# Moving the routing steps of a mixture-of-experts kernel inside its attention stage

## The chip, the cores and the metric

The kernel runs on one core of a Trainium2 chip. A core has five engines that work side by side: TensorE (matrix products, PE in the rows), VectorE (DVE), ScalarE (ACT), GpSimd (POOL) and SyncE (SP), and 16 DMA engines. Each engine takes its instructions strictly in the order of its own queue; an instruction whose operands are not ready holds all that is queued behind it. The metric is the device time of one execution in microseconds.

## The reference

Three stages in a row. The first is a gated linear attention over 4 batches, 8 heads, 768 positions and 48 columns a head:

```python
for t in range(S):
    state = alpha[:, :, t, :, None] * state + k_t (x) v_t
    y[:, :, t] = q_t . state
```

Its output is a matrix of 3072 tokens by 384. The second stage sends each token to two of 8 experts: `logits = x @ w_gate`, plus `log1p(exp(x @ w_noise)) * noise`; the two largest of each token are taken, a softmax over the two gives their weights, and the output is the weighted sum of `relu(x @ w1[e]) @ w2[e]` (384 to 1024 to 384). The third is `(x @ w_a * (x @ w_b)) @ w_out` (384 to 1536 to 384).

## The kernel before

**Attention.** Time is cut in 24 chunks of 128 tokens, six to a batch. In a chunk `i` TensorE does, in this order: the transposes of the next chunk's keys (`t_unit`, line 665), the transposes of the previous chunk's output for the gate (`gx_unit`, line 763), the product of the carried state with the queries (`inter`, line 701; none in the first chunk of a batch), the next chunk's scores (`sc_unit`, lines 681 and 682), masked scores by values (`intra`, line 710), the gate products (`gm_unit`, line 772) and the products of the next state (`u_unit`, line 739). VectorE masks the scores (line 685; the mask is applied to blocks of 128 rows by 64 columns on the diagonal), and makes the two scans of the decays three chunks ahead (`prep`, lines 641 and 645). GpSimd multiplies keys and queries by them (lines 643 and 646), then multiplies the state by its decay (line 755, in `s_unit`), and splits one chunk of expert weights in two parts (line 116). ScalarE copies the output, the state into the layout that `inter` reads (`sbd`, line 728), the masks' result (lines 690 and 692) and transposes out of PSUM.

From chunk `FILL` on, a product of constants (128x128 by 128x512, bf16, line 629) is put ahead of the key transposes and ahead of the gate transposes.

**Routing** is written as Python generators that are advanced by `tick`. There are four ticks in a chunk: 0 behind the transposes, 1 behind the scores and `prep`, 2 behind the masked values and gate products, 3 behind the state. A `yield` ends the generator's share of a tick, so that the number of yields between two steps says how many ticks lie between them. What a step issues goes into the engines' queues at that place of the program. Behind the attention there are two more ticks, then two in each up product (`up_unit`) of the first expert and one in each quarter of a down product.

Tokens are routed in two groups, chunks 0 to 13 and 14 to 23. The second group's choice is made in two parts (chunks 14 to 18, 19 to 23). For a group, `choose` computes the noisy logits and the two best experts, `route` ranks the tokens within each expert with a scan and products of triangular masks (lines 346 to 352), and finds with one-hot products (line 394) the token numbers of expert 0's rows; `gather` (line 494) fetches these rows with an indirect DMA issued by GpSimd, so that `x_unit(0, 0)` to `x_unit(0, 2)` (line 502) can transpose them in and behind chunk 23. `lists` does the same with one-hot products (line 461) for the other experts, in sets of five tiles. `before_states` holds a step that uses TensorE until tick 2 of a chunk, or until no chunk is running.

The first group's steps stand in these places (chunk.tick):

| step | engine | before |
|---|---|---|
| softplus: abs, exp, log, ... | ScalarE | 14.3, 15.0, 15.1 |
| three products, two products | GpSimd | 15.3, 16.0 |
| sum, best and second expert | VectorE | 17.0 to 18.1 |
| sum of both choices; scan | GpSimd; VectorE | 18.2; 19.0 |
| ranks | TensorE | 20.2 |
| rank arithmetic, masks of keys | VectorE | 20.3, 21.0 |
| two lane comparisons (line 385) | VectorE | 21.1, 21.2 |
| places (line 394) | TensorE | 22.2 |
| row indices; three gathers | VectorE; GpSimd | 22.3; 23.0 |
| slot products (line 408) | GpSimd | 23.1, 23.3 |
| lists | VectorE, TensorE | from the second tick behind the last chunk |

The second group's first part has its three and two GpSimd products in 20.3 and 21.0, and its comparisons in 22.0 to 23.1.

**Behind the attention** the eight experts follow, each with up products (lines 846 to 848, three products of split operands), relu and split (lines 897 and 898), and down products; then the third stage. These two take from 140 us to the end.

Of the kernel before, what the change touches and what calls it, by code (L numbers as in the profile page):

```python
# [21 lines left out]
NT = B * NCH  # L22
# [20 lines left out]
LAG = 3  # L43
# [2 lines left out]
W_LOAD = range(4, 20)  # L46
W_SPLIT = [*range(6, 22)]
WARM = 7
FILL = 13
RING = 6  # L50
BLK = 512
NB = N // BLK
# [9 lines left out]
def moe_kernel(ctx: ExitStack, tc, qka, afirst, v, wgn, noise, w1, w2, w3, out):  # L62
# [4 lines left out]
    def tl(pool, shape, dt, tag, **kw):  # L67
        uid[0] += 1
        return pool.tile(shape, dt, tag=tag, name=f"{tag}_{uid[0]}", **kw)
# [91 lines left out]
    def trbank():  # L161
        trn[0] += 1
        return bank(trn[0] % 2)
# [33 lines left out]
    def scratch(name, shape, late, dt=F32):  # L197
        if late:
            return tl(rt, [128, *shape], dt, "s_" + name)
        if name not in SMALL:  # L200
            SMALL[name] = place(shape, None, dt)
        return SMALL[name]
# [33 lines left out]
    def spot(kind, n):  # L236

        c = SPOTS[kind]
        return small[0][:, c:c + n] if small else trbank()[:, :n]

    phase = [None]

    def before_states():
        while phase[0] in (0, 1, 3):
            yield

    def choose(s):

        i0, i1 = CHS[s], CHS[s + 1]
        g, j0 = group_of[i0]  # L250
        n = i1 - i0
        sh = [128, n, E]
        last = i1 == NT

        def tmp(name):
            return tl(rt, [128, MCH, E], F32, "r_" + name)[:, :n]

        def scr(name, *shape):
            return scratch(name, (n if last else MCH, *shape), last)[:, :n]

        def hop(usual, late=0):

            return range(late if last else usual)

        eng = nc.vector if last else nc.gpsimd
        lg, z = LG[:, i0:i1, :E], LG[:, i0:i1, E:]
        az, ex, w, c, r, ln, mz, sp = (tmp(x) for x in ("az", "ex", "w", "c", "r", "ln", "mz", "sp"))
        for _ in hop(1):
            yield
        nc.scalar.activation(az, z, AF.Abs)  # L270
        nc.scalar.activation(ex, az, AF.Exp, scale=-1.0)
        nc.scalar.activation(w, ex, AF.Copy, bias=1.0)
        for _ in hop(1):
            yield
        nc.scalar.activation(ln, w, AF.Ln)
        nc.scalar.activation(r, ln, AF.Exp, scale=-1.0)
        for _ in hop(1):
            yield
        nc.scalar.activation(c, w, AF.Copy, bias=-1.0)
        nc.scalar.activation(mz, z, AF.Relu)  # L280
        for _ in hop(2, 1):
            yield
        eng.tensor_tensor(c, c, ex, op=ALU.subtract)
        eng.tensor_tensor(c, c, r, op=ALU.mult)
        eng.tensor_tensor(sp, ln, c, op=ALU.subtract)
        yield
        eng.tensor_tensor(sp, sp, mz, op=ALU.add)
        eng.tensor_tensor(sp, sp, noise_t[:, i0:i1], op=ALU.mult)
        for _ in hop(4):
            yield  # L290
        nl = scr("nl", E)
        nc.vector.tensor_tensor(nl, sp, lg, op=ALU.add)
        ms = []
        for k in range(2):
            eq = scr("eq", E)
            m, mk = (tl(rt, [128, MCH], F32, f"r_{x}{k}", bufs=2)[:, :n] for x in ("m", "mk"))
            o = oh[k][:, i0:i1]
            nc.vector.tensor_reduce(m, nl, axis=AX.X, op=ALU.max)
            for _ in hop(1):
                yield  # L300
            nc.vector.tensor_tensor(eq, nl, m[:, :, None].to_broadcast(sh), op=ALU.is_equal)
            nc.vector.tensor_tensor(eq, eq, prio[:, None, :].to_broadcast(sh), op=ALU.mult)
            for _ in hop(1):
                yield
            nc.vector.tensor_reduce(mk, eq, axis=AX.X, op=ALU.max)
            nc.vector.tensor_tensor(o, eq, mk[:, :, None].to_broadcast(sh), op=ALU.is_equal)
            yield
            if k == 0:
                nl2 = scr("nl2", E)
                nc.vector.scalar_tensor_tensor(nl2, o, -1e30, nl, op0=ALU.mult, op1=ALU.add)  # L310
                nl = nl2
            ms.append(m)
        oav = oas[g][:, :, 1:].rearrange("p e j -> p j e")[:, j0:j0 + n]
        eng.tensor_tensor(oav, oh[0][:, i0:i1], oh[1][:, i0:i1], op=ALU.add)
        eng.tensor_tensor(dm[:, i0:i1], ms[1], ms[0], op=ALU.subtract)
        for _ in hop(2, 1):
            yield

    def route(g):
# [5 lines left out]
        last = g == len(groups) - 1  # L325
# [12 lines left out]
        nc.vector.tensor_tensor_scan(xc.rearrange("p e j -> p (e j)"), d0[g].rearrange("p e j -> p (e j)"),  # L338
                                     oa.rearrange("p e j -> p (e j)"), 0.0, op0=ALU.mult, op1=ALU.add)
        carry[0] = xc[:, :, n]  # L340
        for _ in range(LAG + 1 if last else LAG):
            yield
        yield from before_states()
        pb = spot("ranks" if last else "ranks0", n * E + E + 1)
# [38 lines left out]
        for j0 in range(0, n, m):  # L383
# [2 lines left out]
                                    op=ALU.is_equal)  # L386
            ats.append(at)
            yield
        for _ in range(LAG - 1 if last else LAG):
            yield  # L390
        yield from before_states()
        pl = spot("lists" if last else "places0", NJ)
# [23 lines left out]
    def hot_tile(name, w, m):  # L416

        size = {"at": 128, "eqk": WL, "bt": WL}[name]
        t = tl(rt, [128, size * 2 * HOT], F16, name, bufs=2)
        return t[:, :w * m].rearrange("p (w t) -> p w t", t=m)  # L420

    def lists(g):

        i0, i1 = groups[g][0], groups[g][-1] + 1
        n = i1 - i0
        pi, ki, pf, kf = (tl(rt, [128, max(GROUPS), 2], dt, x)[:, :n]
                          for x, dt in (("ei", I32), ("ri", I32), ("rf", F16), ("e1", F16)))
        nc.vector.tensor_scalar(pi, slot[:, i0:i1], 127, None, op0=ALU.bitwise_and)
        nc.vector.tensor_scalar(ki, slot[:, i0:i1], 7, None, op0=ALU.logical_shift_right)
        nc.vector.tensor_copy(pf, pi)  # L430
        nc.vector.tensor_copy(kf, ki)
        sets = [(a, b) for a, b in zip(SUBS, SUBS[1:]) if i0 <= a < i1]
        hot = {}

        def make(s):
            j0, j1 = s
            m = j1 - j0
            at, eq, bt = (hot_tile(x, w_, 2 * m) for x, w_ in (("at", 128), ("eqk", WL), ("bt", WL)))
            for out_, src, val in ((at, lane, pf), (eq, keys[:, NJ:], kf)):
                w_ = src.shape[1]  # L440
                nc.vector.tensor_tensor(out_, src[:, :, :2 * m],
                                        val[:, j0 - i0:j1 - i0].rearrange("p a k -> p (a k)")[:, None, :]
                                        .to_broadcast([128, w_, 2 * m]), op=ALU.is_equal)
                yield
            nc.vector.tensor_tensor(bt, eq, token[:, j0:j1].rearrange("p a k -> p (a k)")[:, None, :]
                                    .to_broadcast([128, WL, 2 * m]), op=ALU.mult)
            hot[s] = m, at, bt

        yield from make(sets[0])
        for s, after in zip(sets, sets[1:] + [None]):  # L450
            if after:
                yield from make(after)
            else:
                for _ in range(LAG - 1):
                    yield
            m, at, bt = hot.pop(s)
            yield from before_states()
            pl = spot("lists", WL)
            for j in range(m):
                for k in range(2):  # L460
                    nc.tensor.matmul(pl, at[:, :, 2 * j + k], bt[:, :, 2 * j + k], start=j + k == 0,  # L461
                                     stop=j == m - 1 and k == 1)
            yield
            nc.vector.tensor_tensor((idx if s[1] == NT else lacc)[:, NJ:], pl, lacc[:, NJ:], op=ALU.add)
        yield
# [22 lines left out]
    def gather(e, j):  # L488

        m = min(128, CAP - 128 * j)  # L490
        t = tl(rows, [128, DM], F32, "row")
        a = e == 0 and j < CAPA // 128
        ix = idx[:m, e * NJ + j:e * NJ + j + 1] if e else idx0[:m, j:j + 1]
        nc.gpsimd.indirect_dma_start(out=t[:m], out_offset=None, in_=xd[:SPLIT * 128] if a else xd,  # L494
                                     in_offset=bass.IndirectOffsetOnAxis(ap=ix, axis=0))
        gat[e, j] = t
# [68 lines left out]
    def routing(s):  # L565
        yield from choose(s)
        g = group_of[CHS[s]][0]
        if CHS[s + 1] == groups[g][-1] + 1:
            yield from route(g)
            yield from lists(g)  # L570
        if CHS[s + 1] == NT:
            for q in range(NJ):
                gather(1, q)
                yield
            yield from weights()
# [9 lines left out]
    with ExitStack() as actx:  # L585
# [74 lines left out]
        def t_unit(i):  # L660
            pk = trbank()
            if i >= FILL:
                fill(pk)
# [94 lines left out]
        def gx_unit(i):  # L758
            px = PX[i] = trbank()
            if i >= FILL:  # L760
                fill(px)
# [322 lines left out]
    for e in range(1, E - 1):  # L1084
# [20 lines left out]
        for i in range(2 * KD):  # L1105
            h, k = divmod(i, KD)
# [247 lines left out]
```

## Time and profile before

| | |
|---|---|
| median of 3 runs | 1018.97 us (1016.44 to 1019.65) |
| the profiled execution, its own time | 1018.03 us |
| its span, first to last instruction | 1016.2 us |
| TensorE busy, share of the span | 991.0 us, 98% |
| VectorE, ScalarE, GpSimd busy | 548.4, 401.8, 420.5 us |
| attention ends, experts begin | 140.6 us |

The span is what the trace shows; the execution's own time has 1.8 us around it. A busy TensorE is not one at its peak: its granted clock (PEclk, 1.00 is 2.4 GHz and 0.50 is 1.2 GHz) must be read beside it. In the timelines a bracket says how long the engine had been idle ahead of the row, and what released it.

### The profile page before, as it was taken

The page shows a single profiled execution, that of the slowest core. Times are in us where ns is not written, and L with a number is a line of the kernel's source. Part 1 is how long each engine was busy: PE and PEld are TensorE (multiplying, and loading weights), DVE is VectorE, ACT ScalarE, POOL GpSimd, SP SyncE. Part 2 cuts the span into 40 slices and gives each one's busy share as a digit, 9 for nine tenths or more (in the row PEclk, how much of TensorE's full clock was granted, in tenths as well). Part 3 has the DMA queues.
Part 4 walks back from the last instruction along what each step waited for, and adds up shares of the span by engine and source line. Part 5 has one row for each costly group of instructions (what it writes and reads, how often), then busy time and mean ns, then how long its engine had stood idle before and what let it go on. Part 6 is the DMA issues. An engine that isn't in the chain of part 4 may idle for free.

```text
span 1016.2 us, 18179 instructions
## 1 busy us (share of the span) xinstructions
PE 991.0 (98%) x6928; PEld 897.3 (88%) x6928; DVE 548.4 (54%) x968; ACT 401.8 (40%) x883; POOL 420.5 (41%) x435
## 2 busy tenths in 40 slices
PE   7999979999999999999999999999999999999997
PEld 5988869999999999999999888888888888888886
DVE  8877854676667776667755454332333332333321
ACT  4677631554545454455444243222222222222112
POOL 8688711685868685867674335020020020000000
PEclk9999989999999999999999999999999999999999
DMA  8786210668686868696956535131140140120100
GB/s 314 278 295 256 101 40 28 201 193 241 212 238 215 231 213 241 199 258 207 232 160 189 143 117 132 32 108 16 47 110 1 48 109 1 32 62 1 32 1 34
DMA packets 126552, 141.49 MB, mean 139 GB/s; under 512 B 76512, under 2 KB 110432, under 8 KB 126432
## 3 DMA queue, kind: packets, MB, share of 16 engines
q1 hardware_dynamic: 119904, 120.13, 39.5%
q0 software_dynamic: 6528, 19.67, 6.6%
q8 instruction: 86, 1.41, 0.6%
q14 instruction: 34, 0.28, 0.1%
HBM read 101.43 MB, written 38.34 MB: 138 GB/s over the span
## 4 chain that ended last, share of the span: by engine, by line
PE 83%; DVE 2%; DMA 2%; ACT 1%; issue 1%; POOL 0%; DVEq 0%; POOLq 0%; ACTq 0%
PE bank L846 27%; PE bank L848 27%; PE bank L847 26%; DMA row<-xd,idx 2%; PE bank L502 1%; PE bank L710 1%; PE bank L461 0%; DVE HB L898 0%; PE bank L681 0%; PE bank L701 0%; PE bank L629 0%; ACT o L1188 0%; DVE u L997 0%; PE bank L772 0%; DVE W L116 0%
## 5 line engine op out<-in xcount | busy, mean ns | idle before, releaser
L846 PE MATMUL bank<-HB,W 128*128 128x416 f32 (+5 forms) x564 | 201.4, 357 | 0.7 <-DVE idx L398 0.7
L848 PE MATMUL bank<-HB,W 128*128 128x416 f32 (+5 forms) x564 | 199.9, 354 | 0.0
L847 PE MATMUL bank<-HB,W 128*128 128x416 f32 (+5 forms) x564 | 199.8, 354 | 0.0
L116 POOL TENSOR_TENSOR W<-wst,W 128x384 fp32r<-128x384 f32 x136 | 148.6, 1102 | 85.7 <-ACT W L115 79.5
L1165 DVE TENSOR_TENSOR p<-bank,a 128x512 f32<-128x512 f32 x72 | 49.8, 692 | 236.0 <-PE bank L848 236.0
L846 PE MATMUL bank<-X,W 128*128 128x416 f32 (+6 forms) x474 | 166.5, 351 | 2.7 <-DVE HB L898 2.3
L848 PE MATMUL bank<-X,W 128*128 128x416 f32 (+5 forms) x474 | 165.3, 349 | 0.0
L847 PE MATMUL bank<-X,W 128*128 128x416 f32 (+5 forms) x474 | 165.3, 349 | 0.0
L1027 POOL DMA_INDIRECT row<-y,row x48 | 47.2, 984 | 200.6 <-DVE row L1035 166.9
L846 PEld LDWEIGHTS bank<-HB,W 128*128 128x128 f32 x564 | 106.0, 188 | 8.5 <-ACT HB L897 0.8
L848 PEld LDWEIGHTS bank<-HB,W 128*128 128x128 f32 x564 | 105.9, 188 | 7.4
L847 PEld LDWEIGHTS bank<-HB,W 128*128 128x128 f32 x564 | 106.0, 188 | 7.2
L1163 ACT ACTIVATE a<-bank 128x512 f32<-128x512 f32 x72 | 43.0, 597 | 169.2 <-PE bank L848 169.2
L1167 ACT ACTIVATE HB<-p 128x512 fp32r<-128x512 f32 x72 | 45.5, 632 | 157.0 <-DVE p L1165 157.0
L897 ACT ACTIVATE HB<-bank 128x416 fp32r<-128x416 f32 (+2 forms) x128 | 65.5, 516 | 96.7 <-PE bank L848 96.7
L846 PEld LDWEIGHTS bank<-X,W 128*128 128x128 f32 x474 | 89.1, 188 | 7.6 <-DVE HB L898 3.2
L848 PEld LDWEIGHTS bank<-X,W 128*128 128x128 f32 x474 | 89.0, 188 | 3.9
L847 PEld LDWEIGHTS bank<-X,W 128*128 128x128 f32 x474 | 89.0, 188 | 3.7
L898 DVE SCALAR_TENSOR_TENSOR HB<-bank,HB 128x416 fp32r<-128x416 f32 (+2 forms) x128 | 72.4, 582 | 34.3 <-ACT HB L897 34.0
L494 POOL DMA_INDIRECT row<-xd,idx x56 | 57.8, 1033 | 48.2 <-DVE r_t L408 24.5
L115 ACT ACTIVATE W<-wst 128x384 fp32r<-128x384 f32 x144 | 72.0, 515 | 13.4 <-DMA wst<-w 12.6
L1168 DVE TENSOR_TENSOR HB<-p,HB 128x512 fp32r<-128x512 f32 x72 | 49.9, 692 | 50.3 <-ACT HB L1167 50.3
(243 smaller groups left out, 1852.0 us busy)
## 6 DMA issues: line engine op xcount, KB each, us to landing
wst<-w SPq DMA_DIRECT2D x128, 192.0 KB, 4.6
ring<-qka SPq DMA_DIRECT2D x22, 768.0 KB, 6.2
wd<-w SPq DMA_DIRECT2D x36, 384.0 KB, 5.0
y<-o SPq DMA_DIRECT2D x56, 156.0 KB, 3.0
xt<-tb SPq DMA_DIRECT2D x11, 768.0 KB, 4.5
raw<-xt SPq DMA_DIRECT2D x44, 192.0 KB, 4.6
w3f<-u SPq DMA_DIRECT2D x36, 192.0 KB, 3.3
wst<-w3f SPq DMA_DIRECT2D x36, 192.0 KB, 2.9
```

The lines of the kernel that those rows point to most:

```text
L115: nc.scalar.activation(h, raw, AF.Copy)
L116: eng.tensor_tensor(l, raw, h.bitcast(F32), op=ALU.subtract)
L494: nc.gpsimd.indirect_dma_start(out=t[:m], out_offset=None, in_=xd[:SPLIT * 128] if a else xd, in_offset=bass.IndirectOffsetOnAxis(ap=ix, a ...
L846: nc.tensor.matmul(ps[:, :m], ah, bh[:, :m], start=first, stop=False)
L847: nc.tensor.matmul(ps[:, :n], ah, bl[:, :n], start=False, stop=False)
L848: nc.tensor.matmul(ps[:, :n], al, bh[:, :n], start=False, stop=last)
L897: nc.scalar.activation(Hh[:, f, s], pu[:, :n], AF.Relu)
L898: nc.vector.scalar_tensor_tensor(Hl[:, f, s], pu[:, :n], 0.0, Hh[:, f, s].bitcast(F32), op0=ALU.max, op1=ALU.subtract)
L1027: nc.gpsimd.indirect_dma_start(out=t, out_offset=None, in_=src, in_offset=bass.IndirectOffsetOnAxis(ap=row[:, i, k:k + 1], axis=0))
L1165: nc.vector.tensor_tensor(p, ps[1], a, op=ALU.mult)
L1167: nc.scalar.activation(h, p, AF.Copy)
L1168: nc.vector.tensor_tensor(l, p, h.bitcast(F32), op=ALU.subtract)
```

## The change

`FILL` goes from 13 to 17: no constant products for chunks 13 to 16. In `choose`, for all but the last part, ScalarE's steps take one tick less, GpSimd's products follow behind them with one tick less, and the six steps of the two choices are put in two ticks. `route` of the first group waits one tick less before the ranks and one less before the places. In `lists` the wait for tick 2 goes, and each list product but the last is put two ticks later. `routing` starts `lists` only when no chunk is running, which is the first tick behind the last chunk.

The steps' new places follow from the yields:

| step | before | after |
|---|---|---|
| softplus on ScalarE | 14.3, 15.0, 15.1 | 14.3, 15.0 |
| three products, two products, GpSimd | 15.3, 16.0 | 15.1, 15.2 |
| sum, best and second expert | 17.0 to 18.1 | 16.1, 16.2 |
| sum of both choices; scan | 18.2; 19.0 | 16.2; 16.3 |
| ranks | 20.2 | 17.2 |
| rank arithmetic, masks of keys | 20.3, 21.0 | 17.3, 18.0 |
| two lane comparisons | 21.1, 21.2 | 18.1, 18.2 |
| places | 22.2 | 19.2 |
| row indices; three gathers | 22.3; 23.0 | 19.3; 20.0 |
| slot products | 23.1, 23.3 | 20.1, 20.3 |
| lists | second tick behind the chunks | first tick behind them |
| second group, first part: GpSimd products | 20.3, 21.0 | 20.1, 20.2 |
| its comparisons | 22.0 to 23.1 | 21.1, 21.2 |

The mask on the diagonal blocks is in both kernels alike.

```diff
-FILL = 13
+FILL = 17
...
         nc.scalar.activation(r, ln, AF.Exp, scale=-1.0)
-        for _ in hop(1):
-            yield
         nc.scalar.activation(c, w, AF.Copy, bias=-1.0)
         nc.scalar.activation(mz, z, AF.Relu)
-        for _ in hop(2, 1):
+        for _ in hop(1, 1):
             yield
...
         eng.tensor_tensor(sp, sp, noise_t[:, i0:i1], op=ALU.mult)
-        for _ in hop(4):
+        for _ in hop(3):
             yield
...
             nc.vector.tensor_reduce(m, nl, axis=AX.X, op=ALU.max)
-            for _ in hop(1):
-                yield
             nc.vector.tensor_tensor(eq, nl, m[:, :, None].to_broadcast(sh), op=ALU.is_equal)
             nc.vector.tensor_tensor(eq, eq, prio[:, None, :].to_broadcast(sh), op=ALU.mult)
-            for _ in hop(1):
-                yield
             nc.vector.tensor_reduce(mk, eq, axis=AX.X, op=ALU.max)
             nc.vector.tensor_tensor(o, eq, mk[:, :, None].to_broadcast(sh), op=ALU.is_equal)
-            yield
+            if k == 0 or last:
+                yield
...
         eng.tensor_tensor(dm[:, i0:i1], ms[1], ms[0], op=ALU.subtract)
-        for _ in hop(2, 1):
+        for _ in hop(1, 1):
             yield
...
         carry[0] = xc[:, :, n]
-        for _ in range(LAG + 1 if last else LAG):
+        for _ in range(LAG + 1 if last else LAG - 1):
             yield
         yield from before_states()
...
             ats.append(at)
             yield
-        for _ in range(LAG - 1 if last else LAG):
+        for _ in range(LAG - 1):
             yield
         yield from before_states()
...
             m, at, bt = hot.pop(s)
-            yield from before_states()
+            if s[1] != NT:
+                yield
+                yield
             pl = spot("lists", WL)
...
             yield from route(g)
+            while phase[0] is not None:
+                yield
             yield from lists(g)
```

## Rows read from the trace of the kernel before

**Rows 1.** The chain that ended last, share of the span by engine.
```profile
PE 83%; DVE 2%; DMA 2%; ACT 1%; issue 1%; POOL 0%; DVEq 0%; POOLq 0%; ACTq 0%
```

**Rows 2.** Busy windows: us, busy by engine (instructions), PEclk, DMA share, GB/s.
```profile
130.00:140.00 10.00, 6.99 (x60) 5.12 (x60) 3.18 (x13) 2.93 (x7) 3.29 (x7) 0.67 0.31 100
```

**Rows 3.** TensorE's timeline, chunk 23: start, us, engine, line, output, inputs [idle, releaser].
```profile
128.93 1.03 PE L701 MATMUL bank<-Sbd,ring 128*128 128x96 f32 x8
132.38 0.59 PE L502 MATMUL bank<-ident,row 128*128 128x128 f32 x3 [2.42 <-DMA row<-xd,idx]
133.60 0.88 PE L502 MATMUL bank<-ident,row 128*128 128x128 f32 x3 [0.63 <-ACT X L504]
...
140.61 0.45 PE L846 MATMUL bank<-X,W 128*128 128x384 f32 x1
```

**Rows 4.** TensorE's timeline, chunks 17, 21 and 22.
```profile
95.53 0.39 PE L629 MATMUL bank<-junk 128*128 128x512 bf16 x1
95.76 0.60 PE L665 MATMUL bank<-ident,ring 128*128 128x128 f32 x4
...
96.74 1.03 PE L701 MATMUL bank<-Sbd,ring 128*128 128x96 f32 x8
...
99.91 0.49 PE L772 MATMUL bank<-wgn,gx 128*64 128x16 f32 x12
...
119.26 1.03 PE L701 MATMUL bank<-Sbd,ring 128*128 128x96 f32 x8
...
124.24 1.03 PE L701 MATMUL bank<-Sbd,ring 128*128 128x96 f32 x8
```

**Rows 5.** GpSimd's timeline, chunks 15 to 23.
```profile
94.66 0.43 POOL L283 TENSOR_TENSOR r_c<-r_c,r_ex 128x112 f32<-128x112 f32 x1
...
113.51 1.28 POOL L643 TENSOR_TENSOR ring<-ring,D 128x512 f32<-128x512 f32 x1 [0.95 <-issue]
...
117.82 1.27 POOL L643 TENSOR_TENSOR ring<-ring,D 128x512 f32<-128x512 f32 x1
...
120.44 0.51 POOL L755 TENSOR_TENSOR sc<-ss,aend 128x192 f32<-128x192 f32 x1
120.90 0.27 POOL L283 TENSOR_TENSOR r_c<-r_c,r_ex 128x40 f32<-128x40 f32 x1
...
122.85 0.72 POOL L287 TENSOR_TENSOR r_sp<-r_sp,r_mz 128x40 f32<-128x40 f32 x1
...
129.02 1.14 POOL L494 DMA_INDIRECT row<-xd,idx  x1 [2.58 <-DVE bank L310]
...
132.67 0.44 POOL L408 TENSOR_TENSOR r_t<-oh,r_rs 128x112 f32<-128x112 f32 x1
```

**Rows 6.** VectorE's timeline, chunks 17 to 21.
```profile
97.97 1.34 DVE L292 TENSOR_TENSOR bank<-r_sp,LG 128x112 f32<-128x112 f32 x1
...
99.53 0.74 DVE L685 TENSOR_TENSOR pm<-bank,causal 128x256 f32<-128x256 f32 x2
...
102.98 0.26 DVE L301 TENSOR_TENSOR bank<-bank,r_m 128x112 f32<-128x112 f32 x1
...
118.73 0.17 DVE L357 CAST bank<-bank 128x14 int32<-128x14 f32 x1
...
122.10 2.01 DVE L385 TENSOR_TENSOR at<-lane,r_pf 128x896 f16<-128x896 f16 x2
```

**Rows 7.** ScalarE's timeline, chunk 16.
```profile
95.77 0.73 ACT L728 ACTIVATE Sbd<-sc 64x192 f32<-64x192 f32 x2
```

**Rows 8.** TensorE's timeline, the first expert's up products.
```profile
146.26 1.09 PE L461 MATMUL bank<-bt,at 128*128 128x49 f16 x10 [1.19 <-DVE bt L445]
...
150.59 1.09 PE L461 MATMUL bank<-bt,at 128*128 128x49 f16 x10 [1.13 <-DVE lacc L464]
```

**Rows 9.** Costliest groups of the page: busy us, mean ns | idle before.
```profile
L897 ACT ACTIVATE HB<-bank 128x416 fp32r<-128x416 f32 (+2 forms) x128 | 65.5, 516 | 96.7 <-PE bank L848 96.7
...
L898 DVE SCALAR_TENSOR_TENSOR HB<-bank,HB 128x416 fp32r<-128x416 f32 (+2 forms) x128 | 72.4, 582 | 34.3 <-ACT HB L897 34.0
```

## The prediction

> **What bounds the kernel now.** I read the chain that ended last first, then the busy windows, then the timeline of each engine between 70 and 180 us. TensorE holds 83% of the chain [rows 1], so a change to the routing pays only where it takes away a wait of TensorE or a half-speed stretch. Between 130 and 140 us there are both: TensorE is busy 6.99 of 10 us and its granted clock averages 0.67 [rows 2]. Chunk 23 begins its state product at 128.93; the first transposes of gathered rows begin only at 132.38, after 2.42 us without work that a gather ended; then 0.63 us more pass before 133.60, and the first expert's products begin at 140.61 [rows 3]. A mean of 0.67 over 10 us is 3.3 us lost, so some 6.6 us ran at 1.2 instead of 2.4 GHz. Behind that, two products of the list of places wait 1.19 and 1.13 us for VectorE [rows 8]. Those three places are what the change can win.
>
> **Constant products.** Eight of 128x512 go (one before the transposes of chunks 13 to 16 and one before the gate transposes of the same four). One takes 0.23 us from its start to that of the next work (95.53 to 95.76 [rows 4]): 1.8 us in all. Not all of it comes back: where TensorE must wait for another engine within the chunk, a filler covered a wait that stays. The bounds are 0 and 1.8; I take 1.1 us by the time chunk 16's scores end and 0.2 us more in chunk 17. On the clock their loss costs nothing as long as no longer wait of TensorE takes their place.
>
> **The choice, two ticks earlier on GpSimd.** The five operations on 112 columns now stand in chunk 15 ahead of that chunk's state product instead of behind it. At about 0.46 us each (the first takes 0.43 [rows 5], and the next starts a little after its end) they push the end of that product, after which the first of them starts at 94.66, to 94.66 - 0.9 (the fillers gone by then) + 2.3 = 96.05. ScalarE copies that state at 95.77 before, 94.7 now if nothing held it [rows 7]; it waits until 96.1, needs 0.75, and chunk 17's state product, 96.74 before and 95.4 by the fillers alone [rows 4], begins at 96.9. New wait of TensorE: 1.5 us.
>
> **The choice and scan in two ticks on VectorE.** Chunk 16's scans end, and the sum of logits and noise begins, at 97.97 - 1.1 = 96.85 [rows 6]. That sum took 1.34 us there; the reductions and comparisons behind it are of the same width and take some 0.3 each (0.26 and a handover, row of 102.98). I take 0.5 for the sum (bounds 0.3 and 1.34) and 3.3 for the eleven others; then GpSimd adds both choices, one more operation of 0.43, and VectorE scans the sum, of like width: with the two handovers an estimate of 1.0. The scan ends at 101.65, and GpSimd, which waits at that addition, holds behind it a weight split and the keys of chunk 20; those need a scan that VectorE makes later anyway. The rank products now stand in chunk 17 behind the gate products, which end at 99.91 + 0.49 = 100.40 before [rows 4], now 100.40 - 1.3 + 1.5 = 100.6. TensorE waits 1.0 us more.
>
> **Why did the big sum take 1.34 us?** It ran while GpSimd multiplied; a comparison on the same 112 columns, with one operand fewer in SBUF, takes 0.26 [rows 6]. The Trainium skill, SBUF — State Buffer, Who interferes with whom, says that a VectorE instruction with two SBUF inputs and a GpSimd instruction that reads SBUF shut each other out for the whole instruction. The row agrees; by the rule each moved operation of that kind can cost a GpSimd multiplication. It is rival 3 below.
>
> **VectorE up to the places.** From 101.65 it does, with no pause: mask and both scans (99.53 to 102.98, 3.45 us [rows 6]), a state product (an estimate of 0.3), the rank arithmetic, the masks of keys and the next chunk's mask (118.73 to 122.10, 3.4), that chunk's scans (3.45 less the mask's 0.74, 2.7), and both lane comparisons (2.0 beside GpSimd): 11.9 us, so the second comparison ends at 113.55. TensorE, with 1.4 us of ranks moved in here, comes to the places products a little earlier and waits. The fourteen places products and those of the next state (estimates of 0.75 and 0.5, bounds together 1 and 1.5) then put chunk 20's begin at 114.85.
>
> **GpSimd in chunk 20, the step that decides.** After 113.55 VectorE needs 2.4 us (a state sum 0.3, the mask 0.74, a scan 1.3 with its handover) until GpSimd can start the keys of chunk 22: 116.05 against 113.51 [rows 5]. From there to the keys of chunk 23 it is 4.31 us (113.51 to 117.82). Now three gathers come first, 3.65 us (129.02 to 132.67); then chunk 23's own products, 2.62 (117.82 to 120.44); then, ahead of the state product and no longer behind it, the first slot product (0.44, at 132.67), five operations of the second choice (three as at 120.90, 0.27 and a handover each, 1.0; two more between 0.6, as those, and 1.6, two as at 122.85 with 0.72; I take 0.65); and the state itself, 0.5 (120.44). Sum 13.2: it ends at 129.2, where it ended at 120.9. The gathers' own transfers cross little: the window that holds them before has a DMA share of 0.31 [rows 2]. ScalarE copies that state until 130.0. TensorE would come to chunk 22's state product at 114.85 + 2 x 4.98 (119.26 to 124.24, one chunk) + 1.21 (95.53 to 96.74, a chunk's begin to its state product) [rows 4] = 126.0: it waits 4.0 us. So the 2.42 us wait for a gather is gone from chunk 23, and a longer one stands in chunk 22.
>
> **From there to the experts.** State product to state product it is 4.7 us as before (124.24 to 128.93): the places products are gone from it, but ScalarE's copies need that time. Chunk 23 took 11.68 us (128.93 to 140.61); without 3.05 of waits and 3.3 of half clock 5.3 remain. The experts begin at 130.0 + 4.7 + 5.3 = 140.0: 0.6 us sooner than 140.61 at full clock.
>
> **Clock.** Half clock came right behind 3.05 us of waits in 3.7 us [rows 2, 3]; 4.0 us in one piece should bring it again. Its price is at most the 3.3 us of before, at least 0. I take 2.0, since ScalarE's waits within those 10 us cover a part. The Trainium skill, TensorE: Matmul & The Clock Gate, HAM oscillation, also says that idle gaps of TensorE send the clock to half speed; the rows at 130 to 140 us agree.
>
> **Lists.** They begin two ticks sooner and each product stands two ticks behind its masks, so the 1.19 and 1.13 us go [rows 8]: -2.3. But the third list product moves to the tick before the places of the second group, which share its bank: those must wait until VectorE, behind the last split of an up product, has added the list. ScalarE's relu takes 0.52, VectorE's split 0.58 in the mean [rows 9], the addition some 0.2: a new wait of 0.9 to 1.3, less what TensorE takes to end. Net -1.3 (bounds -2.5 and 0). The second group's lists come two ticks later; their gathers are for expert 1, far behind.
>
> **Sum.** -0.6 + 2.0 - 1.3 = 0.1: against the profiled execution's own 1018.03 us, 1018.1; its span is 1.8 below that, and the median of three runs, 1018.97, 0.9 above. I forecast 1018.0, no change that a measurement can tell: 0.3% is 3 us.
>
> **Rivals.** (1) GpSimd's queue has room after all: the state product of chunk 21 is in time, TensorE never waits 4 us and keeps its clock. Then chunk 22's state product begins at 126.0, chunk 23's 4.7 later at 130.7, and the experts 5.3 behind that, at 136.0 against 140.61: -4.6, lists -1.3, so 1012. For it speaks that the gathers start only 2.6 us behind the last weight split of before [rows 5], so GpSimd has free time late in the attention; against it that these 13.2 us of operations stand in a row and only 2.5 us of slack stood behind the state. 0.26. (2) The wait comes, the clock stays: -0.6 - 1.3, 1016; 0.17, mostly within 0.3%. (3) Shut-out between VectorE and GpSimd grows with the packed ticks: the sum 1.34 instead of 0.5, the last two of the second choice 1.6 instead of 0.65, each gather 1.3 us more while VectorE scans: 3 to 6 us later at the state product, 1021 to 1024; it decides slower from 4 us on. 0.14. (4) The change leaves the wait of chunk 23: not possible unless the gathers' index came late, and it comes three chunks earlier; not priced beyond the range.
>
> **How the numbers follow.** My forecast 0.43, rivals as given. Faster by over 0.3%: rival 1, and a fifth of rival 2, 0.30. Slower: most of rival 3, 0.13. Same 0.57. The likeliest case's own range is 1015 to 1021 (clock 0 to 3.3, lists -2.5 to 0); the whole, leaving out the ends of rivals 1 and 3, 1011 to 1022.
>
> **What would show it.** Right: constant products first at 95 us; a wait of 1 to 2 us before chunk 17's state product and one before the ranks; gathers of GpSimd in a row ahead of chunk 23's key product; TensorE idle some 4 us before chunk 22's state product, released by ScalarE's state copy behind GpSimd's state, and half clock after it; no wait for a gather before the first row transposes; no wait before the first two list products, one before the second group's places. Wrong: if the state of chunk 21 leaves GpSimd before 126 us, or the experts begin before 137 us, the backlog that I summed isn't there, and rival 1 holds.

## The result, and the profile after

The changed kernel takes 1023.67 us (median of 6 runs, 1022.26 to 1025.64) where the kernel before, run beside it, takes 1018.91 us (6 runs, 1016.44 to 1019.71): a ratio of 1.0051 with an interval of 1.0036 to 1.0066. It is slower by 4.8 us, above the forecast of 1018.0 and above the range to 1022. The profiled execution took 1024.07 us, its span is 1022.2 us.

First the busy windows of the changed kernel from the last quarter of the attention to the first experts (us, busy of PE, PEld, DVE, ACT, POOL, then PEclk, DMA share, GB/s).

```profile
100.00:110.00 10.00, 8.77 (x134) 7.24 (x135) 9.03 (x29) 4.49 (x11) 5.34 (x8) 0.83 0.47 159
110.00:120.00 10.00, 9.73 (x225) 8.98 (x223) 8.98 (x17) 7.60 (x26) 8.65 (x10) 1.00 0.18 61
120.00:130.00 10.00, 6.86 (x125) 5.71 (x119) 3.49 (x9) 4.48 (x14) 8.88 (x16) 1.00 0.32 102
130.00:140.00 10.00, 10.00 (x104) 8.86 (x106) 3.94 (x17) 5.93 (x16) 2.33 (x5) 0.54 0.00 0
140.00:150.00 10.00, 10.00 (x105) 9.15 (x106) 7.44 (x26) 4.60 (x15) 0.00 (x0) 0.94 0.11 42
...
160.00:170.00 10.00, 8.14 (x47) 7.90 (x46) 3.54 (x14) 0.49 (x1) 3.78 (x4) 0.83 0.24 69
```

Before, one window had a PEclk clearly below 1.00, 0.67 between 130 and 140 us [rows 2]. Now there are four. Between 130 and 140 us TensorE is busy all of the time and yet slow, for the clock is 1.2 GHz for most of it. In windows of 0.2 us the half clock lasts 6.8 us before (from 133.4), and after it lasts 3.4 us (from 103.4), 10.2 us (from 130.8) and 3.4 us (from 165.0).

TensorE's timeline shows what it did ahead of each of these (start, us, engine, line, operation and tiles; in brackets the idle time ahead of the row and its releaser).

```profile
95.31 1.13 PE L700 MATMUL bank<-Sbd,ring 128*128 128x96 f32 x8 [0.64 <-ACT Sbd L727]
...
101.23 0.39 PE L341 MATMUL bank<-xc,ones 128*128 128x8 f32 x2 [2.12 <-DVE xc L333]
...
113.77 0.86 PE L389 MATMUL bank<-bt,at 128*128 128x7 f16 x14 [0.27 <-DVE ss L753]
...
126.79 0.49 PE L762 MATMUL bank<-ident,x 128*128 128x128 f32 x3
129.98 1.22 PE L700 MATMUL bank<-Sbd,ring 128*128 128x96 f32 x8 [2.70 <-ACT Sbd L727]
...
138.46 1.49 PE L499 MATMUL bank<-ident,row 128*128 128x128 f32 x6
...
144.02 0.44 PE L845 MATMUL bank<-X,W 128*128 128x384 f32 x1
...
162.34 0.71 PE L389 MATMUL bank<-bt,at 128*128 128x7 f16 x10 [1.28 <-DVE lacc L461]
163.63 0.41 PE L845 MATMUL bank<-HB,W 128*128 128x384 f32 x1 [0.57 <-DVE r_t L403]
```

The wait for a gather, 2.42 us in chunk 23 [rows 3], is gone: the transposes of gathered rows at 138.46 have no idle time ahead of them. In its place TensorE waits for chunk 17's state, for the scan ahead of the ranks, and 2.70 us ahead of chunk 22's state product. The experts begin at 144.02 against 140.61 [rows 3]. Further on, the places of the second group wait 1.28 us for the addition of a list.

GpSimd's timeline names what is late in chunk 22.

```profile
118.77 0.51 POOL L754 TENSOR_TENSOR sc<-ss,aend 128x192 f32<-128x192 f32 x1
119.23 1.00 POOL L116 TENSOR_TENSOR W<-wst,W 128x384 fp32r<-128x384 f32 x1
120.40 1.13 POOL L491 DMA_INDIRECT row<-xd,idx  x1 [0.17 <-issue]
121.84 0.95 POOL L491 DMA_INDIRECT row<-xd,idx  x1 [0.30 <-issue]
123.09 0.95 POOL L491 DMA_INDIRECT row<-xd,idx  x1 [0.30 <-issue]
124.06 1.28 POOL L642 TENSOR_TENSOR ring<-ring,D 128x512 f32<-128x512 f32 x1
...
126.68 0.41 POOL L403 TENSOR_TENSOR r_t<-oh,r_rs 128x112 f32<-128x112 f32 x1
127.06 0.26 POOL L281 TENSOR_TENSOR r_c<-r_c,r_ex 128x40 f32<-128x40 f32 x1
...
128.66 0.51 POOL L754 TENSOR_TENSOR sc<-ss,aend 128x192 f32<-128x192 f32 x1
```

From one state (118.77) to the next (128.66) GpSimd has no pause worth the name: three gathers (120.40 to 124.06), chunk 23's own products, a slot product, five products of the second choice, and only then the state, for which ScalarE and TensorE wait. The two VectorE rows that matter are the sum and the scan:

```profile
95.59 1.21 DVE L290 TENSOR_TENSOR bank<-r_sp,LG 128x112 f32<-128x112 f32 x1
96.84 0.27 DVE L296 TENSOR_REDUCE r_m<-bank 128x14 f32<-128x112 f32 x1
...
100.77 0.41 DVE L333 TENSOR_TENSOR_SCAN xc<-bank,oa 128x120 f32<-128x120 f32 x1 [0.54 <-POOL oa L309]
```

### The profile page after: what moved, and what is told of

Its sections match the earlier page's. It is cut to its first block, busy times and chain, and to the rows that moved or that the text cites. A ratio compares the mean times of both kernels' runs of the same rounds, so it can differ in the third digit from the quotient of the medians.

```text
span 1022.2 us, 18161 instructions
## 1 busy us (share of the span) xinstructions
PE 996.8 (98%) x6920; PEld 902.6 (88%) x6920; DVE 547.8 (54%) x968; ACT 402.2 (39%) x883; POOL 416.1 (41%) x435
## 4 chain that ended last, share of the span: by engine, by line
PE 83%; DVE 2%; ACT 1%; issue 1%; POOL 1%; another core or an unknown queue 0%; DVEq 0%; POOLq 0%
PE bank L845 27%; PE bank L847 27%; PE bank L846 27%; PE bank L499 1%; DVE HB L897 0%; PE bank L458 0%; PE bank L709 0%; PE bank L700 0%; POOL row L491 0%; ACT o L1187 0%; DVE W L116 0%; DVE row L1034 0%; ACT HB L896 0%; PE bank L680 0%
## 5 line engine op out<-in xcount | busy, mean ns | idle before, releaser
L1026 POOL DMA_INDIRECT row<-y,row x48 | 46.0, 959 | 201.4 <-DVE row L1034 167.0
L115 ACT ACTIVATE W<-wst 128x384 fp32r<-128x384 f32 x144 | 71.9, 514 | 16.8 <-DMA wst<-w 15.3
```

Of the source, the lines that this page charges most:

```text
L115: nc.scalar.activation(h, raw, AF.Copy)
L1026: nc.gpsimd.indirect_dma_start(out=t, out_offset=None, in_=src, in_offset=bass.IndirectOffsetOnAxis(ap=row[:, i, k:k + 1], axis=0))
```

## The experiments

**The theory and its rivals.** The theory (A, where an expectation uses a letter): steps moved earlier make GpSimd and VectorE late for the attention, TensorE waits at chunk 17, at the ranks and at chunk 22, and these waits with the half clock behind them are the loss. Rivals: the new order of the lists is the loss; the constant products that are gone are; the half clock falls by execution, whatever the waits; the packed steps collide wherever they stand. One measure takes the executions' different starts out: the time from where TensorE comes to chunk 17's state product (its start less its wait) to the first expert's product, 95.31 - 0.64 to 144.02 = 49.35 us here, and 96.74 to 140.61 = 43.87 us before [rows 3, 4].

| kernel | median, us (runs) | ratio to before, 95% | profiled execution: own time | half clock, 96 to 174 us | chunk 17 to experts |
|---|---|---|---|---|---|
| before, twice | 1018.91; 1015.18 | | 1018.03; 1014.30 | 6.8; 6.8 | 43.87; 43.27 |
| after, twice | 1023.67 (6); 1021.33 (1) | 1.0036 to 1.0066 | 1024.07; 1021.33 | 17.0; 17.0 | 49.35; 48.86 |
| gathers later | 1021.15 (12) | 1.0011 to 1.0041 | 1021.40 | 6.8 | 43.72 |
| gathers later, old lists | 1019.10 (11) | 0.9989 to 1.0017 | 1019.40 | 6.8 | 44.79 |
| wait filled | 1023.35 (6) | 1.0027 to 1.0060 | 1025.43 | 13.6 | 48.58 |
| old lists | 1023.75 (6) | 1.0033 to 1.0067 | 1018.63 | 6.8 | 46.86 |
| fillers from 13 | 1025.68 (6) | 1.0040 to 1.0091 | 1026.29 | 17.0 | 48.54 |
| moved steps alone | 1023.15 (12) | 1.0026 to 1.0051 | 1022.78 | 13.6 | 47.09 |
| before, fillers from 17 | 1018.75 (11) | 0.9981 to 1.0002 | 1018.90 | 10.2 | 42.53 |
| ranks later, old lists | 1019.43 (12) | 0.9983 to 1.0021 | 1016.67 | 0 | 42.54 |
| the same, fillers from 13 | 1016.97 (12) | 0.9986 to 1.0015 | 1014.82 | 3.4 | 41.77 |
| choice behind the state, old lists | 1020.65 (12) | 1.0034 to 1.0071 | 1020.11 | 17.0 | 50.02 |

Each ratio is to runs of the kernel before on the same chip in the same series; its median there was 1019.18 us for the gathers later, the filled wait, the old lists and the fillers from 13; 1019.26 for the gathers later with old lists, the moved steps, the kernel before with fillers from 17 and the ranks later; 1017.38 for the ranks later with fillers from 13; 1015.18 for the last row and the two second profiles. The half clock is added up from the granted clock in windows of 0.2 us.

**The gathers behind the state.** In `route`, ahead of the loop of gathers, four ticks, which puts them in 21.0 behind chunk 21's state.

```diff
+        if not last:
+            for _ in range(4):
+                yield
         for j in range(*mine.indices(NJ)):
             gather(0, j)
```

> The changed kernel with the three gathers and the slot products behind them four ticks later (gathers in 21.0 instead of 20.0); all else as changed. Theory A (GpSimd's gathers ahead of chunk 21's state make TensorE's 2.70 us wait in chunk 22, and that wait brings the 10.2 us of half clock behind it): the wait before chunk 22's state product falls under 0.7 us, no half clock between 126 and 140 us, the experts begin near 137.5 instead of 144.0, time 1016 to 1019. Theory B (the choice packed on VectorE, with its 2.12 us wait before the ranks and the half clock of 3.4 us there, sets the time, and later waits only take up what it left): experts not before 141, time 1021 to 1024.

Chunk 22's wait and the half clock behind it are gone, and the loss shrinks from 4.8 to 2.0 us. The experts begin at 140.11 in that trace, not at 137.5, and the time is above theory A's range: neither expectation holds whole. GpSimd's timeline, next to that of the changed kernel, shows the state now 1.6 us ahead of the first gather, and TensorE's that the wait for the ranks stayed:

```profile
126.84 0.51 POOL L757 TENSOR_TENSOR sc<-ss,aend 128x192 f32<-128x192 f32 x1
127.31 1.00 POOL L116 TENSOR_TENSOR W<-wst,W 128x384 fp32r<-128x384 f32 x1
128.47 1.13 POOL L494 DMA_INDIRECT row<-xd,idx  x1 [0.17 <-issue]
```

```profile
102.94 0.39 PE L341 MATMUL bank<-xc,ones 128*128 128x8 f32 x2 [2.12 <-DVE xc L333]
...
158.40 0.69 PE L389 MATMUL bank<-bt,at 128*128 128x7 f16 x10 [1.28 <-DVE lacc L464]
```

Its half clock falls behind these two, from 105.0 and from 159.6. So the gathers' place is worth about half of the loss; the other half is earlier and later.

**The wait filled with constant products.** In `gx_unit`, twelve products of constants where chunk 22 waits.

```diff
-                fill(px)
+                fill(px, 12 if i == NT - 3 else 1)
```

> The changed kernel with 12 constant products instead of one ahead of chunk 21's gate transposes, so that TensorE works through most of the 2.70 us wait of chunk 22; nothing else is moved. If the half clock behind the wait is the larger part of its price (theory A, clock): no half clock at 131 us, experts at 140 to 140.7 instead of 144.0, time 1019.5 to 1021. If the wait itself is the price and the clock would fall anyway: experts at 143.5 or later, time 1023 to 1025.

The median is that of the changed kernel, as the second expectation says, but the profile can't decide between the two: in it the clock had already halved at 115.8 and 126.2, ahead of the place that was filled, and the added products hold TensorE up where chunk 22 would not have waited:

```profile
132.51 2.75 PE L628 MATMUL bank<-junk 128*128 128x512 bf16 x11
...
135.43 1.03 PE L700 MATMUL bank<-Sbd,ring 128*128 128x96 f32 x8
```

One thing here speaks against a loss that is mostly half clock. The five runs without a profile have a mean clock of 0.993 to 0.996, where all six of the changed kernel have 0.986 to 0.990, and they are hardly faster (1021.3 to 1025.5 us against 1022.3 to 1025.6). The added products take a part of what the clock gave back; how large a part isn't shown.

**The lists as before.** One line of `lists` (all kernels called "old lists" have it, and the moved steps alone).

```diff
-            if s[1] != NT:
-                yield
-                yield
+            yield from before_states()
```

> The changed kernel with the list products at their old distance (no two extra ticks); the lists still begin at the first tick behind the chunks. Theory: the wait of 1.28 us before the second group's places, the 0.57 behind it and the half clock at 165 us come from the moved list products: they go, a wait of some 1 us before the second list product comes back, time 1.0 to 2.0 us under the changed kernel, 1021.5 to 1022.7. Rival: the later list products are a gain by themselves (no wait before the second product): time 0.5 to 1.5 above the changed kernel.

The median doesn't move (1023.75 against 1023.67). With the gathers later it falls by 2.0 us, though the two intervals still overlap:

> The changed kernel with the gathers four ticks later and the list products at their old distance. Against the kernel with the gathers alone moved (1021.2 us): if the moved list products cost through the 1.28 us wait and the half clock behind it, 1.0 to 2.0 us less, 1019 to 1020.2. If the list products are neutral: 1020.7 to 1021.7.

1019.10 against 1021.15 us, each beside before at 1019.2. The traces say why the new lists bring nothing. From the first expert's products to its first down product it is 19.6 us with them (144.02 to 163.63), and 20.6 us before (140.61 [rows 3] to 161.17). Most of this 1.0 us is the earlier begin and not the new distance: with the lists as before, which there too begin at the first tick, it is 19.8 in the profile of that kernel (144.37 to 164.14) and in that of the ranks two ticks later (138.59 to 158.35). But then, in each of the five profiles with the new lists, the clock halves behind the waits at the places (1.28 and 0.57 us in the changed kernel), from between 159.6 and 167.0 us on, and in none of the nine with the lists as before. (Four of those nine have 3.4 us of half clock earlier in the lists, from between 145.0 and 151.6. A wait of 1.84 to 1.89 us ahead of a list product stands there in five profiles; half clock follows it in three and not in two.)

**The fillers.** The changed kernel with `FILL = 13`, and the kernel before with `FILL = 17`.

> The changed kernel with constant products from chunk 13 again. If the missing products let the clock fall or cost in another way: 2 us or more under the changed kernel, and no half clock at 104 us. If the waits behind (GpSimd's and VectorE's) set the end of the attention, the products are hidden or cost up to 1.1 us: 1023.5 to 1025.

> The kernel before with constant products from chunk 17 instead of 13, nothing else. If they only filled time that TensorE would have worked in: 0.5 to 1.5 us under the kernel before. If they held the clock: half clock between 70 and 100 us and 1 to 3 us above it.

Neither way does it decide: -0.5 us in the kernel before, within its interval (0.9981 to 1.0002), and 2.0 us more in the changed kernel with intervals that overlap. The loss doesn't shrink when the products come back, so the rival of the fillers falls.

**The moved steps alone.** The changed kernel with `FILL = 13` and the lists as before.

> The changed kernel with constant products from chunk 13 and the list products at their old distance, so that against the kernel before only the steps of choice and route (and the lists' first tick) are moved. Theory: the moved steps are the loss; 3 to 6 us above the kernel before, 1022 to 1025. Rival: the loss needs the missing constant products or the moved lists; under 1 us above it.

They, with the lists' begin at the first tick, cost 3.9 of the 4.8 us, with 2.61 us of wait at chunk 22 and 6.8 us of half clock from 131.0.

**The ranks two ticks later.** They come in 18.2, the gathers in 21.0; the lists as before, and in a second kernel `FILL = 13` too.

```diff
-        for _ in range(LAG + 1 if last else LAG - 1):
+        for _ in range(LAG + 1):
```

> The changed kernel with the rank products of the first group one chunk later (four ticks, with all that follows them: gathers in 21.0), and the list products at their old distance. Theory C (two waits are made by steps that are too close: the ranks two ticks behind the packed choice, the gathers ahead of chunk 21's state; each brings half clock in some executions): neither the 2.1 us wait before the ranks nor the 2.7 us wait in chunk 22 comes, the wait of chunk 23 doesn't come back; experts 4 us sooner than with before's own distance from chunk 16 (49.7 us from the constant product of chunk 16), time 1013.5 to 1016.5. Rival (the packed choice on VectorE costs what the gathers save, wherever the ranks stand): 1018 to 1021.

> The changed kernel with the ranks two ticks later (the gathers one behind that), the lists of before, and constant products from chunk 13 again: what is left of the change is the choice's packed and earlier steps. Its sister with 17 as the first chunk had one profile without half clock between chunk 17 and the first expert at 1016.7 us, and runs from 1014 to 1024. If eight more constant products of 0.23 us cover the 1.4 us wait of chunk 17 and hold the clock: runs close together and 1 to 4 us faster than before. If the scatter has nothing to do with them: the same scatter, within 1.5 us of before. If they only cost: 0.5 to 1.8 us slower than before.

The loss is gone, 1.0002 and 1.0001, but nothing is won: 1019.43 us lies in the range of the first expectation's rival, that the packed choice costs what the gathers save, and that rival stands. In the first kernel's profile no window between 90 and 170 us is below 1.00, though TensorE waits there too:

```profile
100.00:110.00 10.00, 9.03 (x182) 7.88 (x180) 9.06 (x22) 6.65 (x19) 7.30 (x11) 1.00 0.46 162
...
120.00:130.00 10.00, 9.58 (x179) 8.17 (x174) 6.24 (x21) 6.43 (x17) 8.12 (x14) 1.00 0.18 61
130.00:140.00 10.00, 8.99 (x122) 7.48 (x121) 5.38 (x16) 6.37 (x20) 3.16 (x7) 1.00 0.24 80
```

```profile
97.49 1.13 PE L698 MATMUL bank<-Sbd,ring 128*128 128x96 f32 x8 [1.44 <-ACT Sbd L725]
...
146.42 1.09 PE L456 MATMUL bank<-bt,at 128*128 128x49 f16 x10 [1.85 <-DVE lacc L459]
```

Its runs scatter from 1014.1 to 1023.8 us, and go with their mean clock: 0.996 to 0.999 in the four fastest, 0.987 to 0.990 in the five slowest. With fillers from 13 the clock is 0.992 to 0.999 in all twelve runs, and they lie within 4.7 us; but the median is level with before, so the fillers seem to narrow the scatter, and win nothing.

**The choice's products behind the state, ranks one tick later, old lists.** This was to be the version without new waits.

```diff
-        for _ in hop(1, 1):
+        for _ in hop(3, 1):
             yield
         eng.tensor_tensor(c, c, ex, op=ALU.subtract)
...
-        for _ in range(LAG + 1 if last else LAG - 1):
+        for _ in range(LAG + 1 if last else LAG):
```

> The changed kernel with the choice's first five GpSimd operations back where the kernel before has them (behind chunk 15's state product), the ranks one tick later (with that the gathers one too) and the lists of before; the packed steps of the choice and 17 as the first chunk with constant products stay. If the loss is only the waits that the moved steps made and the half clock behind them: no wait of 2 us or more between chunk 17 and the first expert, no half clock there, and a time of 1014 to 1017 us against 1019 before. If the loss lies in the clock by itself, which falls in some executions of any kernel: 1018 to 1021 us and scattered runs. If the shorter steps collide on VectorE and GpSimd wherever they stand: above 1021 us.

It is 5.5 us slower than before. Its 1020.65 us and scattered runs would fit the expectation of a clock that falls by itself, but the three ranges were set against 1019 us, and before took 1015.18 beside it. VectorE's and TensorE's timelines show where the packed choice stands now:

```profile
97.48 1.22 DVE L642 TENSOR_TENSOR_SCAN A<-ring,bank 128x512 f32<-128x512 f32 x1
99.00 1.34 DVE L290 TENSOR_TENSOR bank<-r_sp,LG 128x112 f32<-128x112 f32 x1 [0.30 <-POOL r_sp L286]
...
103.49 0.27 DVE L300 TENSOR_TENSOR oh<-bank,r_mk 128x112 f32<-128x112 f32 x1
103.68 0.74 DVE L682 TENSOR_TENSOR pm<-bank,causal 128x256 f32<-128x256 f32 x2
```

```profile
105.60 0.29 PE L678 MATMUL bank<-ring 48*64 48x128 f32 x1 [2.54 <-ACT pm L689]
...
139.50 1.55 PE L497 MATMUL bank<-ident,row 128*128 128x128 f32 x6 [2.52 <-ACT pm L689]
```

The sum and its eleven followers hold VectorE from 99.00 to 103.76, and the mask of chunk 18 comes behind them: TensorE waits 2.54 us, and 6.8 us of half clock follow. The second group's part does the same at 139.5 (2.52 us). So the rival of collisions holds at the two places where the two-tick choice has a mask due behind it in this kernel.

**Both kernels once more.**

> The changed kernel once more, unchanged, for a second profile. If the half clock behind chunk 22 is the answer to the 2.7 us wait there: a wait of 2.5 to 2.9 us ahead of chunk 22's state product again, half clock for 6 us or more before the first expert again, the experts some 55 us behind chunk 16. If the half clock falls by execution: the same wait, and half clock of another length or place, or none.

> The kernel before once more, unchanged, for a second profile. If its half clock behind the wait for the gather is that wait's answer: the 2.4 us wait in chunk 23 and some 6 to 7 us at half clock behind it again, experts some 49.7 us behind chunk 16. If it falls by execution: another length or place.

Both profiles come back. The changed kernel waits 3.39 us at chunk 22, and has its half clock from 103.8 (3.4 us), 131.0 (10.2) and 165.2 (3.4), the same three within 0.4 us; the kernel before waits 2.37 us for the gather and has 6.8 us from 130.0. The row of the wait in the second profile of the changed kernel:

```profile
130.95 1.89 PE L700 MATMUL bank<-Sbd,ring 128*128 128x96 f32 x8 [3.39 <-ACT Sbd L727]
```

In these two pairs, then, the stretches stand behind the waits each time. Which wait brings one is not settled by the program alone. The kernel with the lists as before runs the changed kernel's program up to the end of the attention, and its profile, taken in the fastest of its six runs, shows the same two waits at chunk 17 and at the ranks as the second profile of the changed kernel (1.43 and 0.89 us; 1.44 and 0.89), with no half clock behind them. TensorE then waits at the places and for ScalarE, with 3.4 us of half clock at each (from 117.0 and 127.2), and not at all ahead of chunk 22's state product:

```profile
103.64 0.39 PE L341 MATMUL bank<-xc,ones 128*128 128x8 f32 x2 [0.89 <-DVE xc L333]
...
116.20 0.86 PE L389 MATMUL bank<-bt,at 128*128 128x7 f16 x14 [1.51 <-DVE ss L751]
...
127.40 0.58 PE L626 MATMUL bank<-junk 128*128 128x512 bf16 x1 [1.32 <-ACT LG L774]
...
134.42 1.03 PE L698 MATMUL bank<-Sbd,ring 128*128 128x96 f32 x8
```

The profile of the filled wait shows the same four waits (1.44, 0.90, 1.51 and 1.45 us). So the rival that the half clock falls by execution holds in part: one program has 6.8 us of it up to the experts in one execution and 13.6 in another, and takes 46.86 or 49.35 us from chunk 17 to there.

From chunk 17 to the experts the change costs 49.35 - 43.87 = 5.5 us in the one pair of profiles and 48.86 - 43.27 = 5.6 in the other. If each half clock costs half of its length, up to the experts 3.4 us before and 6.8 after, then 3.4 of the 5.5 us are half clock and 2.1 the waits themselves; that is an estimate, for waits within a half clock hide a part of its price.

## Why the prediction was wrong

**What held.** *GpSimd in chunk 20, the step that decides*: the operations stood in the order that was summed, and the state ended at 128.66 + 0.51 = 129.17 (129.2 predicted; the sum has a slip, for 113.55 + 2.4 is 115.95 and not 116.05, so it gives 129.1); chunk 22's state product began at 129.98 (130.0). TensorE came to it at 126.79 + 0.49 = 127.3 and not at 126.0, so its wait was 2.7 us (3.39 in the second profile), not 4.0. *VectorE up to the places*: both lane comparisons ended at 113.46 (113.55). *Choice and scan*: the scan ended at 101.18 (101.65). The sum took 1.21 us beside GpSimd's multiplications (0.5 taken, 1.34 the bound), and its followers of the same width 0.27, as the row of before had it; in the last variant it is 1.34. The Trainium skill's rule of shut-out (SBUF — State Buffer, Who interferes with whom) agrees with these rows. The two waits at chunk 17 and at the ranks came to 0.64 + 2.12 = 2.8 us and 1.44 + 0.89 = 2.3, with 1.5 + 1.0 = 2.5 predicted. *Constant products*: -0.5 us in the kernel before, not clear of the noise, and nearer to the bound of 0 than to the 1.1 taken. No wait for a gather, and none ahead of the first two list products, as predicted.

**What failed: the step *Clock*.** It put the price of the new half clock at 2.0 us, and bounded it by "the 3.3 us of before". That takes one wait in one place for granted to bring no more than a stretch of the old length. But the wait of 4.0 us was summed in the same text beside 1.5 us at chunk 17, 1.0 at the ranks and 1.1 at the second places, and each could bring its own. By the experts there were 3.4 + 10.2 = 13.6 us of half clock, at most 6.8 us lost where 2.0 was in the sum. It shows most plainly behind the long wait: from chunk 22's state product to the experts the steps give 4.7 + 5.3 + 2.0 = 12.0 us; 144.02 - 129.98 = 14.0 were measured, and 14.0 again in the second profile. From chunk 17's begin to the experts the prediction's steps give 142.0 - 95.4 = 46.6 us; 49.35 and 48.86 were measured. At full clock they give 44.6; the variant with no half clock there and the ranks' wait gone took 42.54. So the clock term was too small by more than the stretch shows, for the other steps were summed too long, by some 2 us against that variant. The bound was no bound. With the places' stretch there were 17.0 us at half clock, at most 8.5 us lost: put in the place of the 2.0, they bring the prediction's sum from 1018.1 to 1024.6 at most, and this execution took 1024.07. That these two are so near is partly luck, for 2.4 us of this execution's loss come at the very end (below), where no step of the prediction lies.

**Lists, mis-sized for the same reason.** The waits of 1.19 and 1.13 us [rows 8] went, and the new one before the places came with 1.28 us, as summed (0.9 to 1.3). Up to the first down product this brought 1.0 us (20.56 to 19.61), most of it by the earlier begin. Then the clock halved from 165.0 for 3.4 us, which the step had not priced, and by 206 us the kernel was 4.7 us behind. The step's -1.3 was 0 in the changed kernel, and a loss of 2.0 with the gathers later.

**The rivals.** Rival 1 is out, the backlog was there. Rival 2 is out too, the clock did not stay. Rival 3 had the side right and one of its terms (the sum), but not the cause: the state was not late beyond the sum. Its condition, 4 us more at the state product, did not come; that the time lies in its 1021 to 1024 is luck.

**What stays open.** Of the 6.0 us between the first two spans, 3.4 are there at the experts, 4.7 at 206 us and 3.6 at 570 us; the last 2.4 come behind the third stage's last ScalarE output, in code that both kernels share, and 0.5 us is left of them in the second pair. How much of the loss is half clock and how much the waits themselves, no run separates. Why the places' wait of 1.28 us brings half clock each time, and 1.44 us at chunk 17 and 0.97 us at chunk 18 in the ranks' variant don't, the runs don't tell.

## What to carry to other kernels

A wait of TensorE can have two prices, its length and a half clock behind it. The second must be priced for each new wait, not bounded by the stretch that the old wait brought; and since it came in one execution and not in another of the same program, one profile doesn't settle it. A step moved earlier stands ahead of work that was in time: list, for each in-order queue, what is now behind it, as the sum over GpSimd did here to 0.1 us, and look for a place behind the nearest product that another engine waits for. Here that place (ranks in 18.2, gathers in 21.0) takes the loss away, and no variant that was run beats the kernel before.

## What the runs showed of the hardware

The same instructions on the same data ran at different clocks in different variants. Between 10 and 20 us, in code that all variants share, the granted clock was 0.83 in both profiles of before and 0.66 in both of after, but 0.56 in the kernel before with nothing changed except fillers that come only later, and 1.00 where the ranks came later:

```profile
10.00:20.00 10.00, 8.15 (x102) 7.12 (x97) 8.62 (x16) 4.32 (x11) 7.07 (x9) 0.56 1.03 410
```

```profile
10.00:20.00 10.00, 9.01 (x129) 7.89 (x121) 8.61 (x16) 3.94 (x10) 6.76 (x9) 1.00 1.03 412
```

These are the windows of the kernel before with fillers from 17, and of the ranks two ticks later. In the two profiles of before TensorE came to chunk 17's state product at 96.74 and at 94.40, 2.3 us apart, which is why the text above compares stretches and not times from the start. And a half clock can outlast its wait by much: 10.2 us behind 2.70 us, while TensorE was busy in every row of it (10.00 of 10 us between 130 and 140); and waits can bring none, as 1.44, 0.97 and 1.85 us did where the ranks came two ticks later.
